# Two interleaved attention layers on one core: a quarter of the numerator tiles multiplied straight out of PSUM

## The chip, the core and the metric

The kernel runs on one core of a Trainium2 chip. Its time is the device time of one execution in microseconds (us); before the change the median of three runs is 454.13 us (452.84 to 454.67). Beside the runs there is one profiled execution, with a record of every instruction. In its views PE is TensorE's matrix product and PEld its load of weights, DVE is VectorE, ACT ScalarE, POOL GpSimd and SP the engine that only issues DMAs. D names the PSUM tiles.

## What is computed

The input x has 2048 tokens of 512 numbers. Two layers, A and B, are applied twice in turn, each to a layer norm of x and with its result added to x:

```python
x = x + _A_ref(_layernorm(x), ...)   # round 0
x = x + _B_ref(_layernorm(x), ...)
x = x + _A_ref(_layernorm(x), ...)   # round 1
x = x + _B_ref(_layernorm(x), ...)
```

Layer A is attention with 32 heads of 16 in four segments of 512 tokens; from the second segment on, each mixes masked softmax attention within the segment with a memory of the segments before. Layer B is linear attention, where the change lies:

```python
phi_q = concatenate([softmax(pq), softmax(-pq)])   # 32 features from 16 per head
phi_k = concatenate([softmax(pk), softmax(-pk)])
kv  = einsum('bhsf,bhsd->bhfd', phi_k, v)          # over all 2048 tokens
z   = einsum('bhsf->bhf', phi_k)
num = einsum('bhqf,bhfd->bhqd', phi_q, kv)
den = einsum('bhqf,bhf->bhq', phi_q, z) + 1e-06
o   = num / den                                    # then o @ wo
```

Because kv is a sum over all tokens, no query of layer B can be finished before the last key of the round is done.

## The kernel before

The 2048 tokens are 16 tiles of 128, four to a chunk. `Kernel.build` (lines 1143 to 1177 hold its loops) writes down, for each round L, the norm and projections of layer A (`a_proj`), its attention (`a_att`), the output projection (`out_proj`), the norm for layer B, and layer B's keys and values (`b_keys`), segment by segment; then `b_query` for each chunk c. At the end of round 0 the queries of layer B run beside the norms and projections of round 1; at the end of round 1 they are the last thing in the kernel.

Each step becomes an operation in a graph: one matrix product of a tile, one activation, one vector instruction or one DMA. Nothing is scheduled while the kernel runs. `Graph.place` (line 157) unpacks `ORDER`, a compressed table that holds three things: the order of all 2904 operations, the engine of each one that could run on more than one (an evacuation of PSUM can go to ScalarE or to VectorE, `evac`, line 358), and the buffer of each of 1479 tiles. `Graph.emit` (line 190) gives each engine its operations in that order, and puts a wait on a semaphore wherever an operation needs another engine's result or a buffer that is still in use. So an engine whose next operation is not ready stands still, whatever lies behind it.

PSUM is cut into four tiles D of 128 x 1024 32-bit numbers (line 447). Every product of every stage goes through one of these four, and one comes free when the last engine that reads it is done.

`b_query` treats one chunk. In short:

- Two projections BQ (TensorE), each followed by two exponentials `qexp`, of q and of -q (ScalarE, 1024 columns each).
- The sums of the softmaxes and the denominators (`Zq` on TensorE); from these the weights of the numerators, by small steps that go to and fro between the engines: `zlA` (two on ScalarE), `zsy` and `zsd` (VectorE, lines 1091 and 1092), `zlB` (two on ScalarE), `zsw` (VectorE, line 1095).
- For each of the four tiles t a numerator N (line 1106): 16 small products into one D tile, 1024 columns, a half for q and one for -q. ScalarE copies it to SBUF in 16 bits (`Nev`, line 1116) and VectorE multiplies the copy by the weights (`nmul`, line 1117).
- The two halves are added (`nadd`, line 1123) and the sum is transposed by a DMA, or TensorE adds and transposes at once (`otp`, line 929) and the result is evacuated (`ote`, line 933). The set `PE_T` says which.
- The output projection and its addition to x (`res`, line 961) for two tiles together, or for one where `SOLO` says so; in round 1 the store follows.

Which way the numerator takes is set by one line: a tile in `COPIED` (line 1200) is copied first; the other branch (line 1120), which no tile uses before the change, multiplies it out of PSUM.

Most activations are recorded under line 351 (`act`), evacuations under line 359 (ScalarE) or 360 (VectorE), products under 326 and 341, transposing DMAs under 364.

Of the kernel before, what the change touches and what calls it, by code (L numbers as in the profile page):

```python
# [1206 lines left out]
c-q~01GFVsvUWsl@4UXZY}>YNSC?&@UAAr8?6Pg!w(WYE=T=W+diBh#f4zULd71ZQ=FYuCUwjcK^W3<=APJ-ZfO=3L2pT{`Xav!rF*Jdu&<vVGa)<%(AU;%sEKnUPKmsTU60$=nr~#!R8?=Cy&<YgP  # L1207
gxpXODnTJA47s2+w1F~E3)(_is0{5OCX|DOPy~uXd*}eQp%@?(hgk3vl!p?~5n@9f=mec15hR8jkQ1svUFZd=AT?O%0(l@Qe1&iD9jd}h2!vPQKnV1P*U$$HyoWR}2-3np0PG6=;V~fggE!C@y1`%=
0?FVBaOe&LAP?rnx9|Zz!Y3FB`S54x0TUoU_JpaJ3x`5(45EzS2ZX=CbX*71Fqj6SfEhRkp29O2gySIyEWLvgm<e*Tx$qobz<MZ&pJ5n`h7Hgc`(X%$(i9j4#jrSzfG@BZ9EuE^U@8p8d61QDgsm_f
hM*s9hEg~Uw!s#NPW^E<tc23&PYjpBcE}2|U?R?d0k{J+tOAZRVG;&nI+zZVF$kAH3>pI`VKr31DJan5L@0*^aTyfFLRbVVVlWoKH82#*V}2-$r=bk4g~GTTD&YzkhI4T^#-z#^3}ay)j)MRgfs<e_  # L1210
j>O4u5ca}8JOmC#q<yd-65%Kepu-S?k!Tkjhgh^5XX8%TgEKKP#-_;RhqG`#?1m&*0QSIm9F3V_3~E%k2$tYtoP!Op2`<8gSPdKE0!$B0F&eDE>Ub9B<3Ti-3Zsz3Q?L?u&;%Td3t=1<WJ_@w9>OZP
lTu?N{0VDdN=SoMu`$NMHCPj)!g<(7YcVRFg9{KBS5kdU&uU?9tcwev9yZ7Q6c01NDoTKXR0mt&8Q6#|u^G0)P1qWb;|W}k8_*w;Vg!tjNAVc8!M1n+{4o@x(Nzee!x(@O@fz%+v$zejv4j{2&*2f=
j9alC?xv%#1!G`ZTum3@612zt7#+hf4y~aG)B$(mDm;U`FeV;>19%!&<1g3|f5ua|9Ft=~$OqY34z>>K(sD|P8Q4k8!#d##3WXh5i1onj*cqc@3aml(=sb48)|8iZ#S7SmT2ePmNl~yBUBt*34I5HT
T1>|vAFD<6sS$O@RMZofP+``9im<qpnv!8J+(Q{zTk4H_=>%kAwJ9F;!ThWp)uC$?pDtl+%*n1(drC-M=rUZ!q!bIUKoaUq8|Vslq7Jl?I?@nIk4>lrHKU<4jBevYyamJQDqf+cbO)PLW4eY{X$0NH
u5=wAVFtX1-Do7;z-*Wa6Vo%yj+yZ$KE{HS1)t+B%z?e=2^M8Ns5=#+-gF<+VNV)Q11TdGrlmBF#?k{^Mx$s9^`X(!kNQ&rT1$Ot06oQ$bRB-7!8C{t(F9sYhbb+UqMvCZt*0Y2i8j+wDoqDy6HTUr
w1qxkPE13IC;~i$H}nWT;#+!wx#<&z!B;H6GPA9ej6UNn%0u5U9TlP5w4Gj2UOGjm=`|gvZFGl@(HFc+muL!=q096dBf=9pN%`q1<zgr30-d3$bdk=|O}IhR=m5J(Z}A{|i65v0J*NBg3bU|x_>rbl
K6*syX)YCG@9_=3pbRvRvf@hunok$lcbY*(sQ`VW2Xv8rqT-a17SJK~kdo73Hk0nrJ3{Kf-qRp<jy_XIHjBRF05+JNCr$%dCVEC$s2Dw`D~w1`3d#$NuCi-P(pS39zR(a>mVgaq`<NnR<!L`F$Ffp6
noSib8xiZuj<L)X2{dJ=Zmc{rbe#2I71&5Ng7swG*>E<R{mh0j#zwIlY$5e#y;w!M$xg6J)R*;VCs}3c!;Y{V)Q??aM_F+;hK*&HSuT>i1pA2;&q?=KNw$aGXL}iEH=qpb#O|<4>=qO3F1yWMG0D!d
Mf94TXLHyic8)z}57=B*mc3wes0#VBhwLS*N&##h3uLEQH40+$nPQqRV1{c}n$=>}X(2O=bIVRM!OyS>><O#QCbFk&3JYeTtPY#XLRdw1A11Ld_5da`hfQOPS!FhxEn#(8XXeLdv8AjFo5^OdMQl1-
&LXg7>?anPtzhF=L}vL)R)s}j<C()(v0bbbYruB1s%$m;z#6iTtR@TK?^q)i$Xl@Y><fFwKCybNC2Pz+v-<2gi@?9KRt$L%_v67lj7Md_-!OmPnyq1PSqwIluVvNPEFP0JV-fju{tF}ioi%4OcqCqq  # L1220
H)SFG8>`OB^CoOE-@+IV<x_ZdzLmvdk@+?jg>Ppycm>{;MddYlMIM{2W9?Wi9*wVOwfP1Xhppvx_(m3&{lYh~GCUsJ!OHSTY%?p)6S3P+pI7Gb*&V3I>+)*63NOK<u>@=<o6Qrm=&S+Xz~}HvyasE?
f8y;~BVLu4;*I%6-iAfzO?XMZiI?Up`DPx2ui^>WRGy4a<1zVMo}AC)N!Uc5f-mArcxt|bPvYBnN<N=&=V|x?o`5grU3o0NoOk0p`7*wcC*;XlBEFQb<|}wpo|2_t&G;IglqKd@cq(?4uj8rNdft-9
=B;=#)|qeNTX_=Rg~#E|`7WM@#pNydZhnZTW%2l7o|ebwy?JY%j<w?*cpKiGC*?hPTmCaY#`p2#yd%%VqriUNgZJWhcqe|B_vP(*AAW=P<C*zQ-k+c11NaGknrG!%_&|P=AK}?}Dt?ro;ko!Deit6|
?ED@K;<@=Ao`dJ%2l!yVmmlQ!_z-@U-{+V3d48E+<k$FUUXWksWB5@1l#k`N_ys<WKjF7|AwG<c=Q;Uso{pd6BY0u{fKT8Lc^)y6=jG3MKAxUG=cD)*@q*_S1^7$8Rpb+|cz*tx=NB3H7oL&7;oF21
Z~0fgUA*H;eB<wVi1^Mwa4kM^5JnW?C`dRWRD9xof{CKsiqD*j9YTmO;V%-1ouU{I5D7(~NF{<rA`w9Zi6kPmNGu|XG$NKrDk6zpGMR`XB8%8!mxwBIh-e~?h#_{%=wi2sDN=~IBDvTjQ;K*Zt;i|j
i@h?P$RTry^dhUsCUVN$BBRJIGK);2fXE_p$wDH7C@cz!{bG+OBKC>ga<3>Yii!%Nj3_3Gi|V3;$RiJklH#B!B`S(TqO7<g^2!>bk~l2NiL0Wf*e1)1Bcig%Cu@nH#CCa9)E4<=9dS$)lm%p6aZTJ5
g=ArQUEC5?L_Kjs6p^<@eNj~ul?_BOc}MJ!$3->KP}~(KL~C(I?39f}6LD4?lx;*)v0pY8%|vP0T$GX3Wm|DTwh-+^Cs9MT6#L{o(OI+?hh!JgL$nedL|1WN6qko(Pti?u6ura|*<F;7y+s9iRQ@dH
iaw&EJSX~!d7_^<FHVYMvZU-UE{Nl@l$<Y4i8}Iu7$EA()8d}2DF=$BVu7e6@5^hlmK-fUi|ewotS!&UF=CK7F9(Z@qOAN$juk`25K&Jq6y@Y%@kP89U&S|3UY?Z8#3^}6EEnn3WszNFP~$`n^-e4i
UDbDyTD=#~MK?8Gd=MZXikvEqsv_&l7viH>A#$ll;)G1A7Ky5If_N;_sVCx-7@}T^VPckeDyE1Aa;T~%Uy06Yw&<dsiPs{V%Bym#Iii5dr}C&lDvNp}@~gorv&yOpswT3K%A|UzjB1p6AbYBYvalMh
PRn7ckz6T?sNrh0I3vfY$zqLYuf{8X*;F=`t3(HNR`yZ>a-!(1F39d`sz5nST$IDb&#I#$`A}YxBSa@PRZUcr#6T4&AIUz7$pLDNnxgutv1)|sCP#_BYNV>9jJzyw$jWNEn6LV)4zj3PpysM8QptHr  # L1230
${C`nx+*8ANvfJErY5W6>L=Ao#*))i6*XNwmRgolT+S3vWOpfK2~}FfmQQ6#HBz*eR@PQCRT))Q%~BOq9N9)zR5esvSzRquj;yI_sXFRsxk!~)&15-MUDs8ivWBjw{N!TQQMQveWo^Agg~?~KzN(`)
hzN46*eK%4Uqk}ANko<FL<!wqK9>pQ8~H+Zk|lLC8K7UvTe5*lBm;GG>8GR1AnmW0s>HIPiYSA13mHScm8JAMxlA=uDdc-uTE~=~<!qHw_K=O$9JN_2S4~t;nM$ryujE>lOtw@_)f#nMHdDW-<Py{-
wMr$CcVuL_StXUha<wA8Lfw_UB-86ubCpG|SL+4WU1V07TDDTzWNRgK1{p~P$&50J1l>kulI?X@`AMRVq(gN?ZFD@@LC2RHR7<IKn3mdVM@P^~Z&V?Ai;AqH=&fppYOA&>R6EsYnO*Ku?NnX;MQ&Gv
^jEoC4c4TXdM%6Ty{ewxulA`us<%9#ifgXY$q+e0_mLy@LDf(Xmwja;onEGqiFE~?R`!!g^awdn&QKNgXEjpR)L+zcc}UgLA7nW_Kz>tSRefDve^)DH3)Mi+mn-EU*;xOio9QMxs&1-B%QCv7E~^*F
Xu6YbrJL)8^04|SN68|3usos`$)b9Q6sn~jrjM!?dbqBvE9s>An2N2F=}YRkI-^dgI6AsMsjBHJ`mBnfzsZ>TvO1+=>2vD5I<2benew`7tuLr6s*O&rZ>U-Fq8cNws?<8APN7rj*|NJ%sK3j2`e&U+
r`2)wD4js}mx=Uf9bc!@h4eC+Uf)w0^c>kk7uG{`Pkmnv)fshH{ZKtnnRGWD&pc9@WqdPNE|zWeIDJh`)Q{D8y-MCxPt+3mOtsVV<XAaD_tRtaSUpZo)z8&<*;y}@lXVvz$4t^w^aPn%$2F7WMA=LC
(L?1e)mvvUS@ctt(Ol4dbyj^*574*tK;2*8)_3$|c~Ac$r|G*|s_A;Iysz`<OM11eZ!YV{I-6Fifyt|9=yN)s*6OCduJh~j`l+6&Z|Gd+p?;#T=|?)Zd7xjYY$k`fqO+T;+Fw1>Yh+GyM`ba?<Z~UM
vYOW_nF&;}OmZ_z$2KSRZI#4WHCvz3NzEIT&rFeXbUO1^r8n7iLGw~2Fgf%)byuC%3C$~&$fPy-O=4qICX>d@)j4$mliFl9smyy-+te|2O&${mrpgbho|z`ed{pyv0nJPaGha`apHxZnM(5Ib%>unx
pV4o1N|Rfk)hWz39i*bFLgu?(sKG>2FLYsprl5YOm+0tfom{Hl>sNZ2UN2|J*SeJ1AY+*2y0j7IqmHShS*c^16*`9cpc@)x9Q8$i)s0MJ<EK{XMY@UEBtL0wKI>mJH=AXsTCKOpbvl+Zrlwh=tqD`L
jAJU92&$N=Y+9IBrnqTpf>jOE+!QetOf%EcY?Nh;pDAjpn~G+;j;tc7vSzI=XLjiF=B19P+L(`KkFI8-sMh9_scJT8e^bSTsGm%1wNtk>dv!Y#Xm{y2YO4&g?af;gS7oprOk$PMemCz-5*1H@U1^f4  # L1240
1!jv`XjYl!W}i-ESD0j~quFZK>#t^!S!xp7P9}lctrMzmW{ZxmI-6xCk#g)-okIE9jrzTLZMNwE^TvEIpG|TVXnLAd>Wf)yQmP=c%d9qQ%r9o0S!*_!-DabSWHy=2CbG$7dzmGsw^?ttnLZ}7-D!51
P#eW;H^Ii(Fw1RUBdxVjO&1fv3fs>x+tqB+5v{+CW&&)8*<+&FU>j<p+vsMm2{Tb_h()_uA2MVkm@M|7?q(v{!=}55Y9pEhW}i_utBq{;>oZ2%{pO&FVGrw=_N+OikC<%sh(2l#=<N1_IjYZ@^X9ZU
W-gh_=D3MvFPb>^XLHhAF*$5p8{76bIqg+*&BU`k%n5VKTsQG;E_=faFgHzZo50>O$8<uQ%-%M~b#gn}oX|r|0h`YbHF<0rJIv&@1??C!&<rw#>>V@K3^pn3U6ax#vG+`2o79doY3+TJ-i|j9%v1Bw
q_&UDWRu@MHWN%bo60^j&&@>h#C)<ZOc6WW6tz>#ep}4GG{x;_JIR!=uS_NT#ZEOPZDl*ce6^+QPxgQ<ZKs*qwu(JytJ>zajICx5+3L2etz*mC@^-qJWh&SPwuY^1N0}D3qOE6Vn3{IB8EI<ShPJ*v
Z0DF(wvlaVkJy=}wQX#h*q*kHZEEM5cD9#oX6Ko<wzr*V``SMCsGV;H+ex;)J!ZSuPPT&`Vkg_qwx8{4r`nFTn;mF}+Wxk?9bl)}X?BnuW`DNR?K|7U&alJndpp98vJ>n$`@xQ}W9=L}-p;bK?Pz<_
ezeE!NITP_1I}E#&Cavm?J2w6ezWuK0=v;Jv@0z+C+s52oW*vN<<1Tp$ysHSIKtU!H(Ti}v8U}Wo77otm2<{McDC5F?$=;|v(#?237ja-8XM?Dcb3_N&RQG8IcK9f#tCw)v)e{<Vmjxo<1Dv{oIQ4h
P3FXMezAT|VrQ?7?X0sGY;xzK^>?n@U?-)M%2{u3*woG?8{(vJF58<nj&sYVah}>MHm;M_d1i0hbk0?q*(v3ucd|I~oE*+Io56WtpWBR1sFTyl<m|IA>_Z#oWOZKJTux~xn{&rLve}*7&SQJmMsV^t
Pi#RauT#b;<lM7moqSF?C!$l>iSOihUfKJ$h_k`Iwnd!+PI>2zE#_2kiaQmZx3+{+$tmd|N6tBO_kZ4)yAgRG@?E(bAcb$tyY-I+?h(;9`TLV^bI<Vi8+xk|eyDbj5Pkp%H}&iJ4>LXoU6~)}-&T=t
3MhR4{k6|i{?ErBlITf7xP`yE^Q)ylSagHKe+2luYgh8`rvB*6k6HW+3H)oN|JKq!83FVG9gZmeaY*oY@Zj&j!2b{)gulV)??C$J0O;Qj{yzcgUm!*Q2~xi<@<D>XAN&cQ|7Ki%P~eY4^zQsOMD@E2
{(A9SHT)wMq~BEv{dxTB=81)W!V4q3`N59^{5HVfO#S8QPc`<Z0{gAa{juHswRsPXa6JDo`1i{DUv<C#6$kzw+V8*Rz;EY&vvTS0D)+y$;r~S&`#;c}@&8y<zxAL0%GQeiUs|hAJO4wS^MBO{{x_C;  # L1250
v4_XZe{J~uA9uW+dC#lJ5SZ^N7npEom_qH|bQp!}^d6uMLk8|MI73n>wea&t3RXygEQ|sG{DcHfexAMX=j!mMF!C7<3HId^Tovx_bxi~b7C0JDz%v~{LEuXU^ZY^d7p^CgN%kW<0HLUuLq6@qQG+Dm
# [45 lines left out]
```

## Time and profile before

| | before |
|---|---|
| median of three runs | 454.13 us |
| the runs | 452.84 to 454.67 us |
| the profiled execution | 452.45 us |
| its span, first to last instruction | 450.7 us |
| TensorE busy, weight loads apart | 426.8 us |
| weight loads busy | 283.0 us |
| ScalarE busy | 421.6 us |
| VectorE busy | 399.4 us |
| GpSimd busy | 58.5 us |
| granted TensorE clock | 1.00 |

A busy time is the union of an engine's instructions. Products are pipelined and their ends are modelled, so TensorE's figure is not a measure of how near it is to its peak. The chain, a view of its own, is followed back from the last instruction: at each step to whatever released it, or else to the instruction before it on its engine. A group is all instructions of one line, engine, operation and shape, with their number, their total and the mean of one in ns. In a row of the timeline, several alike in succession are drawn together (x3), with the time from the first's start to the last's end. The 32 numerator copies run at 204 to 231 us (round 0) and at 419 to 443 us (round 1), and the multiplies at 206 to 251 and 421 to 444 us.

### The profile page before, as it was taken

How to read it: one execution, taken by the hardware profiler on the slowest of the kernel's cores; microseconds unless marked ns; L12 is line 12 of the kernel's file. 1: busy time of each engine (PE TensorE's matmuls, PEld its weight loads, DVE VectorE, ACT ScalarE, POOL GpSimd, SP SyncE). 2: the span in 40 equal slices, each digit the busy share in tenths (PEclk: the TensorE clock that was granted, in tenths of full speed). 3: DMA queues.
4: the chain of work that ended last, by engine and by line, in shares of the span. 5: the costliest groups of instructions: out<-in, count | busy, mean ns of one | idle time of the engine just before them, and what ended most of it. 6: DMA issues, size and time to landing. Idle time of an engine off the chain costs nothing.

```text
span 450.7 us, 26149 instructions
## 1 busy us (share of the span) xinstructions
PE 426.8 (95%) x12085; PEld 283.0 (63%) x12085; DVE 399.4 (89%) x764; ACT 421.6 (94%) x586; POOL 58.5 (13%) x146
## 2 busy tenths in 40 slices
...
GB/s 252 214 168 54 129 122 98 96 109 76 61 71 97 37 46 33 31 1 16 26 109 114 85 97 110 78 98 83 60 34 56 102 50 63 28 25 4 38 97 188
DMA packets 105167, 36.71 MB, mean 81 GB/s; under 512 B 91730, under 2 KB 105058, under 8 KB 105058
## 3 DMA queue, kind: packets, MB, share of 16 engines
...
q0 software_dynamic: 32, 0.02, 0.0%
...
## 4 chain that ended last, share of the span: by engine, by line
PE 53%; ACT 29%; DVE 11%; DMA 3%; issue 2%; POOL 0%; SPq 0%; DVEq 0%; POOLq 0%
PE D L341 35%; PE D L326 18%; ACT p L351 16%; ACT pP L351 11%; DMA p<-p 2%; DVE stats L599 2%; DMA X<-in_A_x_dram 1%; ACT pS L351 1%; DVE pQ L686 1%; DVE X L961 1%; DVE p L1117 1%; DVE pK L360 1%; DVE p L620 1%; DVE p L360 1%; DVE p L675 1%
## 5 line engine op out<-in xcount | busy, mean ns | idle before, releaser
L351 ACT ACTIVATE p<-D 128x1024 bf16<-128x1024 f32 (+1 forms) x256 | 226.2, 939 | 8.5 <-PE D L341 5.0
L351 ACT ACTIVATE pP<-D 128x768 bf16<-128x768 f32 (+2 forms) x192 | 150.4, 831 | 6.2 <-PE D L326 4.9
L326 PE MATMUL D<-pK,pQ 64*128 64x256 bf16 (+6 forms) x1792 | 110.8, 227 | 5.5 <-ACT pP L351 1.6
L326 PEld LDWEIGHTS D<-pK,pQ 64*128 64x128 bf16 x1792 | 64.1, 94 | 39.9 <-ACT pP L351 8.9
L326 PE MATMUL D<-pW,pP 64*128 64x50 bf16 (+1 forms) x3072 | 84.9, 181 | 1.3 <-ACT pP L351 0.5
L326 PEld LDWEIGHTS D<-pW,pP 64*128 64x128 bf16 x3072 | 68.5, 93 | 9.4 <-ACT pP L351 1.4
L607 POOL TENSOR_SCALAR rstd<-mv 128x1 f32<-128x1 f32 x60 | 16.7, 282 | 337.2 <-DVE mv L600 337.2
L326 PE MATMUL D<-pW,p 64*128 64x50 bf16 (+1 forms) x2048 | 49.2, 181 | 0.1
L326 PEld LDWEIGHTS D<-pW,p 64*128 64x128 bf16 x2048 | 43.4, 93 | 3.9 <-ACT p L351 0.5
L599 DVE BATCH_NORM_STATS2 stats<-X 128x6 f32<-128x512 bf16 x63 | 42.3, 681 | 1.9 <-DMA X<-in_A_x_dram 1.4
L961 DVE TENSOR_TENSOR X<-X,D 128x1024 bf16<-128x1024 bf16 (+1 forms) x36 | 39.4, 1098 | 3.0 <-PE D L341 2.7
L326 PE MATMUL D<-tri,rep 64*128 64x64 bf16 (+1 forms) x384 | 39.2, 197 | 0.0
L341 PE MATMUL D<-pX,WA_q 64*128 64x512 bf16 (+1 forms) x288 | 37.5, 353 | 0.2
L341 PE MATMUL D<-pX,WA_k 64*128 64x512 bf16 (+1 forms) x288 | 37.1, 353 | 0.5
L609 POOL TENSOR_TENSOR rstd<-rstd,mhalf 128x1 f32<-128x1 f32 x60 | 36.3, 608 | 4.0
L1015 DVE TENSOR_REDUCE pS<-p 128x64 f32<-128x1024 bf16 x28 | 33.4, 1210 | 1.6 <-ACT p L351 1.6
L341 PE MATMUL D<-WA_o,p 64*128 64x512 bf16 (+1 forms) x288 | 32.9, 353 | 1.8 <-ACT pP L351 1.0
L341 PE MATMUL D<-WB_k,pX 64*128 64x512 bf16 (+1 forms) x288 | 33.5, 353 | 1.0 <-ACT pP L351 1.0
L341 PE MATMUL D<-WB_o,p 64*128 64x512 bf16 (+1 forms) x288 | 32.9, 353 | 1.3 <-DMA p<-p 0.5
L341 PE MATMUL D<-WB_v,pX 64*128 64x512 bf16 (+1 forms) x288 | 33.2, 353 | 0.2 <-ACT p L351 0.2
L341 PE MATMUL D<-WA_v,pX 64*128 64x512 bf16 x256 | 32.9, 377 | 0.1
L341 PE MATMUL D<-pX,WB_q 64*128 64x512 bf16 x256 | 32.2, 377 | 0.1
...
## 6 DMA issues: line engine op xcount, KB each, us to landing
...
p<-p SPq DMA_TRANSPOSE x73, 3.2
pX<-p SPq DMA_TRANSPOSE x54, 3.7
...
```

What stands on the lines that cost most here:

```text
L326: ins = e.matmul(out_ap, lhsT, rhs, start=st, stop=sp, tile_position=(basep(lhsT), basep(out_ap)))
L341: ins = e.matmul(out_ap, lhsT[64 * hf:64 * hf + 64], rhs[64 * hf:64 * hf + 64], start=k == 0 and i == 0, stop=k == 1 and i == len(lists[hf ...
L351: return self.g.op({"act": (dur, lambda e: e.activation(out_ap(), in_ap(), func, scale=scale))}, reads, writes, opens, label=label)
L360: "dve": ((340 if fast else n / 0.96 + 65), lambda e: e.tensor_copy(out_ap(), in_ap()))}
L599: v(lambda e: e.bn_stats(self.stats[:, t, :], self.X[:, t, :]), 602, [R("X", t)], [R("st", t)], label="bn")
L607: v(lambda e: e.tensor_scalar(rs, self.mv[:, t, 1:2], LN_EPS, None, op0=ALU.add), 170, [R("mv", t)], [R("rstd", t)], eng="pool", label="rstd")
L609: v(lambda e: e.tensor_tensor(rs, rs, self.mhalf[:], ALU.pow), 540, [R("rstd", t), R("mhalf")], [R("rstd", t)], eng="pool", label="rstd")
L620: v(lambda e: e.tensor_scalar(xn.t[:], self.X[:, t, :], self.mv[:, t, 0:1], self.rstd[:, t:t + 1], op0=ALU.subtract, op1=ALU.mult), 300, [ ...
L675: v(lambda e: e.tensor_tensor(cut(dst), cut(dst), cut(e_), ALU.min), 68 + n / 1.92, D + E, D, label="phadd", port=True)
L686: ch = {"dve": (129 + n / 3.84, lambda e, sl=sl, out=out: e.tensor_scalar(out(), src(), self.m4[:, sl:sl + 1], None, op0=ALU.mult))}
L961: self.v(lambda e: e.tensor_tensor(X(), X(), src(), ALU.add), 65 + 512 * n / 0.96, pr + xr, xr, label="res")
L1015: v(lambda e, E=E, k=k, Z=Z: e.tensor_reduce(Z.t[:, 64 * k:64 * k + 64], E.t[:].rearrange("p (a f h) -> p a h f", a=16, h=4), AX.X, ALU.ad ...
```

## The change

Of each four numerator tiles the last is taken out of `COPIED`. The eight tiles 3, 7, 11 and 15 of both rounds now take the branch at line 1120: no `Nev` and no copy in SBUF, and `nmul` reads D.

```diff
-COPIED = {(L, t) for L in range(2) for t in range(16)}
+COPIED = {(L, t) for L in range(2) for t in range(16) if t % 4 < 3}
```

The two ways, as they stood and stand:

```python
if (L, t) in COPIED:
    Ns = self.T(self.p2, "T")
    self.act(lambda Ns=Ns: Ns.t[:], lambda N=N: N.t[:], ACT.Copy, 1024, [N], [Ns], label="Nev")
    v(... e.tensor_tensor(shape(Tm.t[:]), shape(Ns.t[:]), w(), ALU.mult) ..., label="nmul", port=True)
else:
    v(... e.tensor_tensor(shape(Tm.t[:]), shape(N.t[:]), w(), ALU.mult) ..., label="nmul")
```

The rest of the diff replaces `ORDER`, 52 lines of text, with a table for the 2896 operations and 1471 tiles that are left. Unpacked and set beside the old one, with the eight copies left out, it has the same operations in a slightly different order: 401 of TensorE's 1165 stand at the same place in its queue, 302 of ScalarE's 569 that both tables give it, 101 of VectorE's 755. The mean shift is 2.3 places on TensorE, 0.9 on ScalarE, 4.9 on VectorE and 2.9 on SP; 1039 of the 1471 tiles get another buffer of their pool. Seventeen operations change their engine (times are those of the profiled execution before):

```
to ScalarE:  ote of tiles 1, 2 (round 0) and 0, 14 (round 1); K of round 1, segment 0 (235.6 us);
             Q of round 1, segment 1 (248.7 us); one accumulation of the memory (263.6 us)
to VectorE:  K of round 0, segment 2 (67.4 us); K and V of round 1, segment 1 (248.8, 270.5 us);
             layer B's V in round 1, three times (362.6, 387.1, 403.3 us);
             one evacuation of a transpose (394.4 us); one mask of K (12.9 us)
to GpSimd:   two memsets of the setup (1.9, 39.2 us)
```

In the last stretch of the kernel the order of the numerators' steps on VectorE becomes, from the first weights on: tiles 3, 1, 2, 10, 8, 11, 0, 9, 5, 7, 4, 12, 6, 13, 14, 15 (before: 3, 2, 1, 10, 0, 9, 11, 8, 5, 4, 7, 12, 13, 6, 15, 14).

More of the change, by code (lines that the diff above doesn't have):

```diff
@@ L1206 @@
 ORDER = """
[L1207 to L1250, printed above, removed]
@@ L1255 @@
-?k9-(nCGGHl9@utbvD!`pmDf6$6Phipuct#=2FAur=RyO3f85G8&RMSBws!-{FT$yBP{-)qA#<;4bNCt7r9jg-n%BFU<$(!aPS8e!AN()-^JI529j~@IvC(_&!ZM-5#ac0ED*v8qCEW`OT9mjgu%Y0
-KEk<o1R1Wvn09Fq#=@1jQW_i<>;>$}xCP*HIMij0^l9*fT@o8N!0=Ewx|t92no6MbaY!(K@PX~C2hUXz;wkdIL;Ezk*F1oQdhV0IuOi*lg}H?SDADJz%fBEuJhw#rJSKT7LOpi4*n1`H`5{Fp_jnQH
-2w&#W@u~K>;R{-@A2jzAcwoA1%lJVsy5;Oc&({e8K)EdEgg<@=Fu^X*1H5GTq`}{<+YmRYzAq8-x}U30yP0F;6}hX__bY>c2m}PX^S~igyU>9v;b;m~#%mc67>2&E$+bin>b5rHqD=lmY7Ag*jBYq?
-xue?vf|S3+0C(Va70|{_1q*gd&8-D4{K%0Qgob;~(5*SwnsCkk4-Bs7x&
+c-rlEWwhkVt*%Nc_U65ZnVFfHnVFfHXU;G)Gcz+YGcz+Y^USk*&q>Zn@^X{4@_yv5=We@PE=eVQ`lNQpfD{0b9P&d-s1F1ZvI0T_P|y%8B!Whe3m7zpoZvtchzW6_Da3=^&<sjK2qb~%&>Rv&AQXgB
@@ new lines @@
+&;qhU1*i@NvOr771EoPgD<}jtpf!|%n$QL~<b$@54GKe9Xa}(%8We%{5FctmMTiYWApj~tIp_ezpf*&7j!+(wK_{pK#i0sxh7!;PK0;mS3iY5W^oH+H4Sv9DNCn;CC!~fx04xo>fdr5i-hzg~z*t|%
+1fL)wAR7P!p*!@0A<!QNK~ne(PvIT(fFKwOdDtlU0{NI9{04bhPk09Jp%+YJ7N0|YmW#cB_3#05Q*M?6GQ&%l!KSkf5QMMbE6ikr*hrWQ8(}aj!RA49EXg*(aOlS-!Z(--6CfCuKz}wLim_=B8AiZp
+m;^&uaW)Jx!gkmUb6_Z&4yD)*I1Q!QGML0>z*g7^#AZPZ%t~8e09yrlXdBE1&hpYgwi<RpOmuK21Tuf{!!b|*mckmC!X`6+6f78mSS*~%LU1oEhqX|E6=j9kSSZ3OuzgUFS+)+!u)?e&E60M_9w^U-
+v9fG8tbpOH5}U_X!hBYljbP(oBpVNtVLyumQ{XThV3LhuXJJ1C;1M_g>0mS~NQu}52w_Jd8|`HWVHVRYG26$|!yI-7X0x&EJQO0s#;~Q#VRKnSmV_-}OIRQ_Volj1wwNu3W~@3>Y$b~dHCRME%oehf
@@ new lines @@
+u!^N(u`wx&ghyB?+l5tF1{lZu*aSA7?Z!ngkyT}paT!a^0$3DW&Z@D()R+~aG^{3T!s4)eREve;3bvLVz;$dPT!gr60bGJ}a1d8vJXVj@Va-_s)`qRdR;(^-%{H@^EGpJ#wOI=mhFjQ17RI9CCU%mw
+Wk*>%c8VQm`6&X6&l0fq>^NM9V=N*&1UKLW+sY!b9V{i=#`fR^mYkhqd+``thCM6}uEEG`JB!X@unz1BM8LHeh3#esSw|L=9b)NeHA}(HvQF$gTf@?_(`-Epg)?je%RmX)3XIL_VP}?+R$_Lli8<&u
+wv+8*^|1@<$=YC7c9HdB-B>M5#xAi|*cMY_Z*~e=<7L(e`>-V#mDR=u*chX+RM?j-#Z1%?<6>$&0sF8Hc4zys9oEHo*n_pl8yFw2u$$=5I$&4qf=MtTUWKdd8pL9o@EU819dR=b#ZK56o8vHSiNmo8
+W@OjdV>SZQvm5L#yM{Me2G#<b;Vm{2uVXiS!tTI5)*bJ&QTTvmW0}|s_K;;~nb}j8gB8Rq>?M1|GE;AS#&S|mEQGgNA54VlSX%6b<1qq^!@{@>$KV|{2$$mo9Eg2!G>*jq*aQ3HI_!rDup~Zbzu|fu
@@ new lines @@
+f`jo0Zor9n6iZ<doP=3uBPPXTxD_YkaXf^HaSI;CWH<%4;U`ua)8IS&%-&-<ybX_GJAP+RAUA$tuUHEF!R}xl{L1cP0eXXZaR=_iGx!!y;ypZzCGZ61WcTq3eq&Ry7+%HV_zZK=X#{+Zr|=S<!)bUK
+&*Lr3$_~+OoR05VQB019=^_4PPw*3dVEHgVrpKc68DF!HtQh^o0{99u;9K?@FW@DL2tP0*KElgX2A|>=JVLkND;}jc>;pc)ckD5K#Ex_kXW(G!L<1=+4k3<+gNX12zC?!CNZ?G&j@M}x-XMwJ@FoqV
+@0bOL(E(BjR2~l!qjFRhD<D!f>_+qO1eHULMBS-889Yhzu_rCS3N)HV(Lx+Uy=Wx$pb^xEexu=Zi!xzFtVFk|63)g`R2lox06I;*DF+^-E7X^cQ-8{g#c3?%#H%!pBridWQ1LK$KqV;`?xTmapE#AJ
+#n_qdQC_%1rAg3znuB+#480*q=jkm)fk!l#=Hf*<NApP0E2@eY=rO&f`SgUU;Tc*$)o~&Dlje)4HfahVLxx-8{3)HKKoZ=ci4;W7s17}+Ni>y$DU_yBT?(O!^bjUf7(Ie1bQ3DmQtCp>C^Ai_uC#<^
```

43 lines of the change are left out of this document (39 added, 4 removed).

## The prediction

> **What bounds the kernel now.** I read the page's busy times and its chain first, then a table of windows, the chain in order of time, the groups of instructions, and single stretches of the timeline.
>
> ```profile
> PE 426.8 (95%) x12085; PEld 283.0 (63%) x12085; DVE 399.4 (89%) x764; ACT 421.6 (94%) x586; POOL 58.5 (13%) x146
> ...
> PE 53%; ACT 29%; DVE 11%; DMA 3%; issue 2%; POOL 0%; SPq 0%; DVEq 0%; POOLq 0%
> ```
>
> Three engines are nearly full, and no one of them sets the end alone: the chain runs 53% over TensorE, 29% over ScalarE, 11% over VectorE. What ScalarE loses is worth time only where the chain lies on ScalarE, and what VectorE gains costs time only where VectorE has no slack. So the next view is the table of windows, cut where the change acts (columns: window and length, then busy us of PE, PEld, DVE, ACT, POOL).
>
> ```profile
> 60.00:80.00 20.00, 18.93 (x544) 13.86 (x538) 17.98 (x38) 19.56 (x28) 6.93 (x14) 1.00 0.78 111
> 200.00:214.00 14.00, 12.09 (x412) 7.57 (x408) 11.15 (x27) 13.89 (x23) 0.00 (x0) 1.00 0.06 12
> 214.00:228.00 14.00, 13.30 (x326) 7.46 (x324) 13.76 (x31) 14.00 (x23) 3.31 (x8) 1.00 0.29 43
> 252.00:300.00 48.00, 46.82 (x1387) 32.00 (x1380) 41.74 (x84) 47.08 (x60) 9.64 (x24) 1.00 0.58 93
> 380.00:410.00 30.00, 30.00 (x710) 18.71 (x708) 23.89 (x39) 26.16 (x42) 3.13 (x8) 1.00 0.18 30
> 421.10:448.20 27.10, 24.25 (x528) 13.31 (x528) 26.61 (x47) 21.40 (x32) 0.00 (x0) 1.00 0.58 120
> ```
>
> The two query stretches of layer B, where all copies of the change lie, are about 200 to 252 and 415 to 448 us. At 200 to 214 ScalarE is full (13.89 of 14.00) and VectorE is not (11.15). At 214 to 228 both are full. In the last 27.1 us VectorE is the fullest of all: 26.61, or 98%. At 380 to 410 it is TensorE (30.00 of 30.00).
>
> **What each piece costs.** From the groups by line:
>
> ```profile
> L1117 DVE TENSOR_TENSOR p<-p,pS 128x1024 bf16<-128x1024 bf16 x32 | 21.4, 686 | 0.4
> L835 DVE TENSOR_TENSOR p<-D,pS 128x1024 bf16<-128x1024 f32 x12 | 14.6, 1217 | 0.9 <-PE D L326 0.4 <-ACT pS L351 0.2
> L360 DVE CAST p<-D 128x1024 bf16<-128x1024 f32 x10 | 12.2, 1221 | 1.1 <-PE D L341 0.9
> L360 DVE CAST p<-D 128x512 bf16<-128x512 f32 x7 | 4.7, 679 | 0.1
> L359 ACT ACTIVATE p<-D 128x512 bf16<-128x512 f32 x6 | 3.6, 596 | 0.6 <-PE D L341 0.4
> L359 ACT ACTIVATE pT<-D 128x1024 bf16<-128x1024 f32 x7 | 7.1, 1037 | 0.0
> L688 ACT ACTIVATE pQ<-p,m 128x512 bf16<-128x512 bf16 x2 | 1.3, 723 | 0.0
> L553 DVE MEMSET pW<- 128x1088 f32 x1 | 1.0, 965 | 0.2 <-issue 0.2
> ```
>
> And from the timeline of ScalarE, three numerator copies in a row, and the first of the last query stretch among its neighbours:
>
> ```profile
> 206.02 2.84 ACT L351 ACTIVATE p<-D 128x1024 bf16<-128x1024 f32 x3
> ```
>
> ```profile
> 417.87 0.38 ACT L351 ACTIVATE pS<-D 128x256 f32<-128x256 f32 x1
> 418.29 0.42 ACT L351 ACTIVATE pS<-pS 128x256 f32<-128x256 f32 x1
> 418.76 1.02 ACT L351 ACTIVATE p<-D 128x1024 bf16<-128x1024 f32 x1
> 419.68 0.30 ACT L351 ACTIVATE pS<-pS 128x128 f32<-128x128 f32 x1
> 419.88 0.38 ACT L351 ACTIVATE pS<-D 128x256 f32<-128x256 f32 x1
> 420.14 0.61 ACT L351 ACTIVATE pS<-pS 128x128 f32<-128x128 f32 x2
> ```
>
> One copy lasts 1.02, but the next begins before it ends: (2.84 - 1.02) / 2 = 0.91 us is what ScalarE gets back for each. VectorE's multiply took 686 ns from SBUF. Before shows none with a numerator in PSUM; the nearest row is L835, the same operation and size with its large operand in PSUM: 1217. I take 1217, so + 0.53 us for each.
>
> **Part 1: eight copies gone.** ScalarE 8 x 0.91 = - 7.3 us; VectorE 8 x 0.53 = + 4.2 us; the wait of a multiply for its copy goes, and a wait for the product itself takes its place. Queued behind that wait on VectorE are, in the table of after, the next tiles' multiplies and half-sums, and behind the last one four residual adds; for these wait the transposes of SP and TensorE, the output projections and the stores.
>
> **Part 2: engines that the new table moves.** Unpacked, the two tables differ in 17 engines. From VectorE to ScalarE go four evacuations of 512 columns (tiles 1 and 2 of layer 0, 0 and 14 of layer 1) and two of 1024 (K at 236, Q at 249 us); from ScalarE to VectorE six of 1024 (K at 67 and 249; V at 270; layer B's V at 363, 387 and 403). One costs ScalarE about 0.5 or 0.9 us, VectorE 0.6 or 1.13 (the rows less an overlap of 0.1). ScalarE: 2 x 0.9 + 4 x 0.5 - 6 x 0.9 = - 1.6. VectorE: 6 x 1.13 - 2 x 1.13 - 4 x 0.6 = + 2.1. Small pieces (a mask, L688, and a 512-column evacuation go to VectorE, an accumulation to ScalarE, a memset, L553, to GpSimd, which is 13% busy) take about 0.7 more off each. Whole kernel: ScalarE - 10, VectorE + 6, TensorE 0.
>
> **Part 3: order and buffers.** TensorE keeps 401 of 1165 steps in their place and the others move by 2 or 3 on the mean (22 at most); ScalarE's by 10 at most. SP's transposes and loads move by 3 places on the mean (some weight loads of the first 60 us by more), GpSimd's setup memsets change places among themselves ahead of its first normalisation step; in the last query stretch two stores go ahead of transposes on SP, which costs nothing, as VectorE's queue has their residual adds ahead of the half-sums that those transposes wait for. I cost the reshuffle at nothing, because the same steps stand in the same stretches; its bounds are in the range. It is the least known term.
>
> **Where it lies on the path.** The chain in order of time, at the places concerned:
>
> ```profile
> 65.88 1.02 ACT p L351
> ...
> 68.01 1.04 PE D L341 x8
> ...
> 210.16 2.74 ACT p L351 x3
> ...
> 214.42 1.17 DVE X L961
> ...
> 362.87 0.96 PE D L341 x8
> ...
> 418.76 1.02 ACT p L351
> ...
> 426.13 1.99 ACT p L351 x2
> ...
> 434.72 1.87 ACT p L351 x2
> ```
>
> - *K at 67 us.* The chain leaves ScalarE for TensorE at 68.01, ScalarE is the fuller (19.56 against 18.93 of 20): between 0 and 0.9; I take half, - 0.45. V at 363 likewise, on the border from TensorE (362.87): - 0.45.
> - *V at 387 and 403, the evacuations at 236 to 270.* Hidden behind TensorE (30.00 of 30.00; 46.82 of 48.00). Nothing, so long as VectorE's slack there (6.1 and 6.3 us) takes them; if it did not, 1.13 us each.
> - *First query stretch.* The chain holds two removed copies (210.16, x3): - 1.8; two 512-column evacuations come to ScalarE ahead of the same point: + 1.0. From 214.42 the chain is VectorE's, which has + 2 x 0.53 and - 2 x 0.6 by then. ScalarE's bound is - 0.8, VectorE's - 0.1; I take - 0.5.
> - *Last query stretch.* ScalarE's bound: three copies on the chain (418.76, 426.13, 434.72), 3 x 0.91 = 2.7, less 0.5 for the evacuation that comes over: - 2.2. VectorE's bound: 4 x 0.53 - 2 x 0.6 = + 0.9 on an engine at 98%. But VectorE also begins earlier:
>
> ```profile
> 420.48 0.43 DVE L1095 TENSOR_TENSOR pS<-pS 128x256 bf16<-128x256 f32 x1 [0.99 <-ACT pS L351]
> ...
> 421.15 0.69 DVE L1117 TENSOR_TENSOR p<-p,pS 128x1024 bf16<-128x1024 bf16 x1
> ```
>
> It stood idle 0.99 us for weights whose last step on ScalarE was queued behind the copy at 418.76. Without the copy that step comes some 0.4 earlier (a second chunk's two steps, 0.2 to 0.6, now go ahead of it), and more of VectorE's small work is done in the gap: 0.7 to 1.0 us. So + 0.9 - 0.9 = 0 for this stretch; the later of the two bounds, VectorE's, decides.
>
> Sum: - 0.45 - 0.45 - 0.5 + 0 = - 1.4 us. The profiled execution took 452.45 us (span 450.7, 1.75 around it), 1.7 below the median shown, 454.13; the same step from the median gives 452.7. What a measurement of this kernel can tell from no change is about 0.5%, 2.3 us, so the forecast is a small gain inside it.
>
> [...]
>
> **Rivals.**
>
> A. *ScalarE's relief pays wherever the chain is on it.* The full terms: - 0.9, - 0.9, - 0.8 and - 2.2 make - 4.8 us: 449.3. At its far end all of ScalarE's 10 us come off: 444. For it: TensorE's waits below, 7.2 us in these three rows alone, end on ScalarE. Against: VectorE's 98% at the end.
>
> ```profile
> PE D L326 <- ACT p L351: 3.1, 9, 0.5
> PE D L326 <- ACT pP L351: 2.1, 9, 0.4
> ...
> PE D L341 <- ACT pP L351: 2.0, 3, 1.0
> ```
>
> B. *VectorE becomes the bound in the query stretches (slower).* A numerator now holds one of four PSUM tiles until VectorE's queue reaches it. The multiply is longer and stands behind residual adds (L961, 1.17 us in the chain above), and TensorE's next product waits for the tile. Price: the + 4.2 of the eight multiplies, with the 4 x 0.6 of evacuations as a credit or, if TensorE then waits for ScalarE's, without it: + 1.8 to + 4.2, up to 458; at the middle, + 3: 457. It decides once VectorE has no gap left to absorb 2 us in the last 27 (it has 0.5 now). Against it: the table puts VectorE's multiplies close behind their products.
>
> C. *The copies are not on the path and nothing moves*: 454, as TensorE's 426.8 us are untouched.
>
> **Chances.** My case with C, -3.4 to + 1 us around - 1.4: 0.46, of which 0.12 lies beyond 0.5% faster. A: 0.32. B: 0.20, of which 0.02 is under 0.5%. What is left, that the change doesn't do what it says, 0.02, counts as the same. Faster by over 0.5%: 0.44; within: 0.38; slower: 0.18. The likeliest case's own range is 450.7 to 455.1. The range for 8 in 10 reaches into A to 447.5, past its 449.3 by the 2 us that the order may give, and into B to its middle, 457.0.
>
> **What would show it.** ScalarE's busy time near 411, VectorE's near 405, TensorE's at 427. L1117 as two forms: 24 of about 686 ns, 8 of about 1217 reading 32-bit D. In the last 27 us VectorE at 98% or more, and the chain there passing from ScalarE to VectorE: right. A chain still on ScalarE there and a span down by over 4: A. TensorE's waits on L1117 or L961 over 3 us in the query stretches: B. A multiply from PSUM far from 1.2 us, or a difference that sits outside the query stretches, makes my working wrong whatever the time.

## The result, and the profile after

After takes 450.06 us (median; 448.93 to 456.62, but for one execution of 687.42 us at a granted clock of 0.56), before 454.32 us (450.17 to 456.8) beside it. The ratio is 0.992 [0.989, 0.994]: faster by 0.8%, 3.8 us, and the interval leaves out no change. The profiled execution took 449.23 us against 452.45, with a span of 447.5 us against 450.7.

The page's busy times and chain:

```profile
PE 426.6 (95%) x12085; PEld 284.3 (64%) x12085; DVE 404.1 (90%) x763; ACT 413.1 (92%) x577; POOL 57.5 (13%) x148
...
PE 63%; ACT 20%; DVE 13%; issue 2%; DMA 1%; DVEq 0%
```

ScalarE lost 8.5 us and VectorE gained 4.7. The chain's share on ScalarE fell from 29 to 20% and went to TensorE. The groups of copies and multiplies:

```profile
L351 ACT ACTIVATE p<-D 128x1024 bf16<-128x1024 f32 x184 | 183.7, 1041 | 7.7 <-PE D L341 4.0 <-PE D L326 3.1
L1117 DVE TENSOR_TENSOR p<-p,pS 128x1024 bf16<-128x1024 bf16 x24 | 15.9, 684 | 0.0
L1120 DVE TENSOR_TENSOR p<-D,pS 128x1024 bf16<-128x1024 f32 x8 | 9.8, 1220 | 0.0
```

The eight multiplies out of PSUM took 1220 ns each (1217 was the estimate). The same windows as before the change, the last one again the 27.1 us up to the last addition to x:

```profile
60.00:80.00 20.00, 19.85 (x538) 14.02 (x539) 19.02 (x35) 19.06 (x28) 3.56 (x7) 1.00 0.77 110
200.00:214.00 14.00, 13.15 (x428) 8.29 (x430) 11.60 (x22) 13.97 (x24) 0.85 (x3) 1.00 0.13 22
214.00:228.00 14.00, 13.62 (x282) 7.39 (x278) 13.79 (x30) 13.93 (x22) 2.38 (x6) 1.00 0.36 81
252.00:300.00 48.00, 46.76 (x1380) 32.29 (x1372) 42.92 (x87) 46.61 (x61) 10.24 (x24) 1.00 0.55 96
380.00:410.00 30.00, 29.77 (x686) 18.95 (x680) 27.27 (x47) 23.42 (x37) 3.15 (x8) 1.00 0.15 25
418.20:445.30 27.10, 23.78 (x512) 12.78 (x512) 25.78 (x42) 18.58 (x30) 0.00 (x0) 1.00 0.58 118
```

TensorE is fuller at 60 to 80 us (19.85 against 18.93) and at 200 to 214 (13.15 against 12.09). In the last stretch VectorE is not fuller but emptier, 25.78 against 26.61. The chain there, in order of time:

```profile
416.89 1.24 DVE p L1120
418.57 1.20 DVE p L1117 x2
421.06 1.01 ACT p L351
422.27 1.83 ACT p L351 x2
...
431.03 1.83 ACT p L351 x2
433.85 1.05 PE D L341 x8
...
440.62 2.19 PE D L341 x24
442.83 1.82 DVE X L961 x2
```

It begins with a multiply out of PSUM on VectorE, goes to ScalarE and from 433.85 us to TensorE's output projections.

Where the time came from is read by laying the two traces over each other: for each operation of ScalarE and VectorE, its end after less its end before, and of these the median in each 20 us. The lead of after is 0.2 us at 20 to 40 us, 1.1 at 40, 1.9 at 60, 2.9 at 180, 3.1 at 200, 3.9 at 240, 3.6 at 300 and 3.3 at the end. So in this pair most of it stood before the first numerator. The experiments were built on that; how far a single pair can be trusted is seen at their end.

### The profile page after: what moved, and what is told of

Read it like the earlier page. It is cut to its first block, busy times and chain, and to the rows that moved or that the text cites. A ratio compares the mean times of both kernels' runs of the same rounds, so it can differ in the third digit from the quotient of the medians.

```text
span 447.5 us, 26142 instructions
## 1 busy us (share of the span) xinstructions
PE 426.6 (95%) x12085; PEld 284.3 (64%) x12085; DVE 404.1 (90%) x763; ACT 413.1 (92%) x577; POOL 57.5 (13%) x148
## 3 DMA queue, kind: packets, MB, share of 16 engines
q8 instruction: 95, 1.56, 1.4%
## 4 chain that ended last, share of the span: by engine, by line
PE 63%; ACT 20%; DVE 13%; issue 2%; DMA 1%; DVEq 0%
PE D L341 39%; PE D L326 21%; ACT p L351 13%; ACT pP L351 6%; PE D L701 2%; DVE X L961 1%; DVE pQ L686 1%; DVE p L360 1%; DVE stats L599 1%; ACT pS L351 1%; DVE pS L1015 1%; DVE p L675 1%; DMA pX<-p 1%; DVE p L620 1%; DVE p L1117 1%
## 5 line engine op out<-in xcount | busy, mean ns | idle before, releaser
L351 ACT ACTIVATE p<-D 128x1024 bf16<-128x1024 f32 (+1 forms) x248 | 217.1, 931 | 11.2 <-PE D L341 7.2
L326 PEld LDWEIGHTS D<-pK,pQ 64*128 64x128 bf16 x1792 | 65.6, 93 | 40.5 <-ACT pP L351 8.1
L326 PE MATMUL D<-pW,pP 64*128 64x50 bf16 (+1 forms) x3072 | 83.6, 181 | 1.2 <-issue 0.7
L326 PEld LDWEIGHTS D<-pW,pP 64*128 64x128 bf16 x3072 | 67.5, 93 | 6.4 <-issue 1.1
L607 POOL TENSOR_SCALAR rstd<-mv 128x1 f32<-128x1 f32 x60 | 15.8, 272 | 338.4 <-DVE mv L600 338.2
L961 DVE TENSOR_TENSOR X<-X,D 128x1024 bf16<-128x1024 bf16 (+1 forms) x36 | 39.0, 1094 | 4.0 <-PE D L341 3.4
L609 POOL TENSOR_TENSOR rstd<-rstd,mhalf 128x1 f32<-128x1 f32 x60 | 35.2, 596 | 2.7
```

The source lines that it names most:

```text
L326: ins = e.matmul(out_ap, lhsT, rhs, start=st, stop=sp, tile_position=(basep(lhsT), basep(out_ap)))
L351: return self.g.op({"act": (dur, lambda e: e.activation(out_ap(), in_ap(), func, scale=scale))}, reads, writes, opens, label=label)
L607: v(lambda e: e.tensor_scalar(rs, self.mv[:, t, 1:2], LN_EPS, None, op0=ALU.add), 170, [R("mv", t)], [R("rstd", t)], eng="pool", label="rstd")
L609: v(lambda e: e.tensor_tensor(rs, rs, self.mhalf[:], ALU.pow), 540, [R("rstd", t), R("mhalf")], [R("rstd", t)], eng="pool", label="rstd")
L961: self.v(lambda e: e.tensor_tensor(X(), X(), src(), ALU.add), 65 + 512 * n / 0.96, pr + xr, xr, label="res")
```

## The experiments

A kernel was put together from the two tables, by order, engines, copies and buffers. Each comparison is with before on the same chip in the same session (453.0 to 455.7 us), so ratios are compared. The theories were: T1, the new order and engines ahead of the query stretches make the gain and the edit nothing; T2, ScalarE's eight copies make it; T3, the edit costs time on VectorE and the order overpays that.

**1. The edit alone, in the old order.**

```diff
 order and engines of before; 48 tiles in other buffers; 6 steps put off for want of a buffer
-32 copies
+24 copies
+the product N of these eight tiles 2 to 7 places before its multiply, where it stood 9 to 111 before it
```

> The edit alone: the eight tiles are multiplied out of PSUM, but order and engines are those of the old table. (The product of a tile that stood more than eight places ahead of its multiply is moved to six places ahead of it, 6 steps are put off by a place or more until a PSUM tile is free, 48 tiles get another buffer.) Theory 1, the gain of 3.8 us is the new order and its engines in the first 197 us, ahead of the first numerator, and the edit is worth about nothing: 453 to 456 us, the last 27 us on VectorE unchanged or up to 1 us longer. Theory 2, the gain is ScalarE's 7.3 us of copies: 449.5 to 451.5. Theory 3, the edit by itself costs time on VectorE and the order overpays it: 456 to 458.

463.85 us, 1.021 [1.016, 1.026]. Slower by 2%, more than any of the three theories expected; T3 is the nearest, as TensorE now waits for the new multiply:

```profile
PE D L341 <- DVE p L1120: 2.9, 3, 1.2
```

**2. The new order and engines, with all copies.**

```diff
 order and engines of after; 50 tiles in other buffers, 8 more for the copies
-24 copies
+32 copies, the eight 2 to 4 places behind their products
```

> The edit undone: order and engines of the new table, but all 32 tiles are copied by ScalarE again; each of the eight copies is put four places behind its product in the order. Theory 1 (the order ahead of the first numerator): 449.5 to 451.5 us, no slower than the changed kernel by over 1.5. Theory 2 (the copies): 453 to 455. Theory 3 (the edit costs): 447 to 449.5, faster than the changed kernel.

457.54 us, 1.007 [1.003, 1.011]: slower than before, and 1.6% above after. This speaks against T1: with all copies put back like this the new order is no gain.

**3. The new table up to the first query step, the old one from there, all copies.**

```diff
-order and engines of before for the first 1360 operations; buffers
+those of after; 53 tiles in other buffers
```

> The first part of the new table alone: its first 1360 operations, up to the first denominator product of layer B in round 0 (about 197 us; the old table has the same operations there but one), then the old order and engines, with all 32 copies. Theory 1: most of the gain, 451 to 452 us, and the span up to the first numerator shorter by 2.5 to 3. Theory 2 and theory 3: 453.5 to 455, and the lead of the first part lost again behind ScalarE in the query stretch.

457.27 us, 1.004 [1.000, 1.008].

**4. The old table up to there, the new one and the edit from there.**

```diff
-order and engines of after for the first 1360 operations; buffers
+those of before; 64 tiles in other buffers
```

> The second part of the new table alone: the old order and engines for the first 1360 operations (about 200 us), then the new order with the eight tiles out of PSUM. Theory 1: 453 to 454.5 us, a gain of 0 to 1. Theory 2: 450 to 451.5. Theory 3: 455 to 457.

454.34 us, 0.998 [0.995, 1.002].

So each mixture lost the gain, and none of the three theories says that. The profiles of runs 2 and 3 have something that they do not mention. Both execute the first 1360 operations in after's order on after's engines, and yet TensorE stood still in the middle of a product, waiting for nothing that the profile shows. First the timeline of run 2, then its windows (busy us by engine as above, then the granted clock, the share of the DMA engines and GB/s):

```profile
60.75 1.02 PE L341 MATMUL D<-pX,WA_q 64*128 64x512 bf16 x7
65.19 0.39 PE L341 MATMUL D<-pX,WA_q 64*128 64x512 bf16 x1 [3.42 <-issue]
```

```profile
60.00:62.00 2.00, 1.40 (x20) 0.59 (x15) 1.97 (x5) 2.00 (x4) 1.97 (x4) 1.00 1.58 251
62.00:64.00 2.00, 0.00 (x0) 0.00 (x0) 0.67 (x2) 0.38 (x2) 0.00 (x0) 1.00 1.74 114
64.00:66.00 2.00, 0.81 (x27) 0.77 (x29) 0.00 (x0) 0.10 (x1) 0.00 (x0) 0.90 0.34 69
66.00:68.00 2.00, 2.00 (x25) 1.54 (x21) 1.60 (x2) 1.41 (x2) 0.00 (x0) 0.50 0.04 8
```

After the gap of 3.42 us the clock stood at 0.50. In run 3 the gap was 3.46 us, up to 66.84, and the clock stood at 0.50 from 66 to 70 us. By the tables run 3 has after's buffers too in these 1360 operations, so the same stretch of program ran with the gap in the one profiled execution and without it in the other. In after the eight matmuls run through:

```profile
60.28 1.54 PE L341 MATMUL D<-pX,WA_q 64*128 64x512 bf16 x8
```

The queue of instruction transfers, q8 in the DMA view, shows the other half. In before, after and runs 2 and 12 it counts 95 packets and 1.56 MB, 16 KB each; TensorE's 24,170 instructions (12,085 products and as many weight loads) make 254 for each, so I take q8 to be TensorE's refill. That is my estimate from these counts: no view names the engine. In after one falls in the window from 55.7 to 60 us, starting at 59.01. In run 2 none falls in 56.7 to 61.8. The queues' rows of these two windows (packets, MB, share of 16 engines), after first:

```profile
q1 hardware_dynamic: 896, 0.59, 57.4%
q8 instruction: 1, 0.02, 1.4%
```

```profile
q1 hardware_dynamic: 1560, 0.97, 100.5%
```

There the data queue had the engines at 100.5%, with a 512 KB load of layer B's weights among it (it stands in after's window too, issued at 57.22 us), and the refill started at 61.88, while the eighth matmul began only at 65.19. In each of the five such gaps of runs 2, 3 and 8 to 10 TensorE went on 1.3 to 1.4 us after the end of the late refill's packet, which bears this reading. T5: it is this collision that made the mixtures slow, not what they were made of. It does not account for run 4, whose profile has no stand of this kind over 0.9 us.

**5 and 6. Engines without order, order without engines.** The other two came out of the same question: which part of the new table is it?

```diff
 run 5: order, buffers and 32 copies of before
-17 operations on their engines of before
+17 operations on their engines of after
```

> The order, the buffers and all 32 copies are those of before; only the 17 operations that the change puts on another engine are on it. If the engines are what was gained ahead of the query stretches (K at 67 us and another early product off ScalarE): 451 to 452.5, with the lead of 1 to 3 us there by 200 us. If they pay only with the order that was made for them: 454 to 457, since nothing stands where the new engine is free. My guess is the second, 455.

457.63 us, 1.009 [1.006, 1.012].

```diff
 run 6: order, buffers and 24 copies of after
-17 operations on their engines of after
+17 operations on their engines of before
```

> The order, the buffers and the edit are those of after; the 17 operations are on their engines of before. If the new order alone carries the gain ahead of the query stretches: 450 to 452, the lead of 3 us still there at 200 us. If the engine changes carry it: 453 to 456, with the lead gone from 67 us on. By theory T2 (ScalarE's relief) it is slower, since the moves of the query stretches put work on ScalarE that the edit has freed: VectorE then keeps the two output transposes and three scalings, +1.8 us on VectorE in the first query stretch.

456.35 us, 1.003 [1.000, 1.006]. Neither half pays by itself. The first query stretch, 196 to 252 us, suggests why, though a fixed window holds slightly different work in each kernel; before, then run 5, then run 6, then after (PE, PEld, DVE, ACT, POOL):

```profile
196.00:252.00 56.00, 52.74 (x1362) 31.59 (x1360) 51.25 (x112) 55.36 (x78) 6.59 (x16) 1.00 0.37 61
```

```profile
196.00:252.00 56.00, 51.94 (x1338) 30.78 (x1340) 47.56 (x102) 55.80 (x79) 6.59 (x16) 1.00 0.41 61
```

```profile
196.00:252.00 56.00, 51.79 (x1348) 30.69 (x1344) 51.60 (x106) 51.36 (x71) 6.19 (x16) 1.00 0.38 60
```

```profile
196.00:252.00 56.00, 53.56 (x1428) 32.53 (x1424) 51.65 (x104) 55.14 (x78) 6.13 (x16) 1.00 0.38 65
```

With the engines moved and the copies kept, ScalarE is full (55.80 of 56) while VectorE has 8.4 us free. With the edit and the old engines ScalarE has 4.6 us free and TensorE does less work. With both, the work that went to ScalarE fills what the copies left, and TensorE does 1.6 to 1.8 us more in the same window, 0.8 us more than before.

**7. The control for run 1.**

```diff
 order, engines and buffers of run 1
-24 copies
+32 copies, each 1 to 3 places behind its product
 one multiply changes places with its neighbour
```

> The control for the edit alone in the old order (463.85): that kernel's order, with the numerator's product moved late, its put-off steps and exactly its buffers, but with all 32 copies, each some three places behind its product. It differs from the edit alone in the eight copies and nothing else. If the multiplication out of PSUM is what cost the edit alone its 10 us: 453 to 456 here. If the late products and the other buffers cost it: 460 to 465.

463.28 us, 1.019 [1.014, 1.024]. Run 1 by run 7: 1.002 [0.995, 1.009]. In this order, the old one with the products moved late, the edit shows no gain and no cost, to within 0.5 and 0.9%; what cost run 1 its 10 us is what I had built around it. T3 has lost its evidence. The edit in before's order as it stood was not run.

**8. The control for run 2.**

```diff
 order, engines and 24 copies of after
-buffers of after
+buffers of run 2 (50 tiles)
```

> The control for the new order with its copies put back (457.54): the kernel after, with exactly that kernel's buffers (50 tiles in other buffers than after). It differs from it in the eight copies and nothing else. If the copies cost it its 7 us against after (theory T2 within the new order): 450 to 451.5 here, as after. If the buffers cost it: 455 to 458, and the mixtures so far say little about copies or order.

453.96 us, 1.000 [0.997, 1.003]. Other buffers alone take after's gain away. Its timeline has the gap at the same matmul, and the refill started at 61.96 us:

```profile
64.45 0.39 PE L341 MATMUL D<-pX,WA_q 64*128 64x512 bf16 x1 [2.05 <-issue]
```

**9 and 10. The load moved away.** Run 9 is run 8, run 10 is after, with one DMA at another place:

```diff
 SP's queue
-load (wqkv, 512 KB)
 PhKtr L0 s1 gp1; vsw L0 s1 gp1; otr L0 s0 i02 gg1; xnT t1; xnT t0
+load (wqkv, 512 KB)
```

> The kernel after with the other buffers (453.96; the profiled run 451.40) with one DMA moved: the 512 KB load of layer B's weights that went out at 57.55 us stands five places later in SP's queue, behind the transpose of 64.5 us. New theory T5: that load kept back the 16 KB refill of TensorE's instructions that is due at about 59 us (it started at 61.96, and TensorE stood 2.05 us with nothing to wait for, 3.4 us in two other runs), and the buffers as such cost nothing. T5 expects 450 to 451.5, no gap of TensorE over 1 us at 62 us, and the refill at 59 to 60 us. If the buffers cost their 4 us through waits of the engines: 453 to 455 as without the move.

> The kernel after, with its own buffers, and the same load five places later. By T5 the profiled run of after was on the good side of that collision (load out at 57.22 us, refill at 59.01 us, no gap), and most of its runs too: 449 to 451, as after (450.06) or a little under it where some of its runs were caught. If the load's late landing (about 70 us, its transposes are issued at 70.65 us) holds something back: 451 to 453.

Run 9: 450.75 us, 0.994 [0.991, 0.997]; run 10: 450.81 us, 0.995 [0.991, 0.998]. With the load moved, the other buffers cost nothing that shows: run 9 by run 10 is 0.999 [0.995, 1.004]. The move itself made the kernel of run 8 faster: run 9 by run 8 is 0.994 [0.990, 0.999]. The refill of run 9 started at 58.04 us, but the gap did not go, it moved with the load; this is the timeline of run 9, and run 10 has the same 1.42 us at 72.30:

```profile
72.10 0.31 PE L326 MATMUL D<-pK,pQ 64*128 64x128 bf16 x6 [1.42 <-issue]
```

**11. Before with other buffers.**

```diff
 order, engines and 32 copies of before
-buffers of before
+54 tiles in other buffers, 27 of them in those of run 7
```

> The kernel before with 54 tiles in other buffers, order, engines and copies untouched: about as many as the edit alone in the old order had (48 to 49). If the buffers cost the edit alone and its control (463.85 and 463.28) their 10 us: 460 or more here. If it is the late products that cost it: 454 to 456, and what is above 454 is the price of buffers not chosen for the order.

455.79 us, 1.006 [1.003, 1.009]. Of run 7's 1.9%, 0.6 may be the buffers, though only 27 of its 49 moved tiles stand here as there; the rest, 1.3% [0.7, 1.9], is then the late products and the steps put off.

**12. The copies back in the new order, without the gap at 62 us.**

```diff
 order (with the load later), engines and buffers of run 9
-24 copies
+32 copies
```

> The new order and engines with all 32 copies (457.54, where TensorE stood 3.42 us at 62 us and its clock fell to half for 3.4 us behind that), with the same 512 KB load five places later. It differs from the run with other buffers and the load later (450.75) in the eight copies and nothing else, and neither has the gap at 62 us. So it prices the edit within the new order, free of that collision. Theory T2 (the copies' time on ScalarE, 8 x 0.91 us, is on the path): 453.5 to 455.5, the loss lying at 200 to 240 us and behind 410 us. If the edit as such is worth nothing (T1): 450 to 451.5, and the whole 7 us by which the copies lost before were the gap and the clock.

458.34 us, 1.006 [1.004, 1.009]. Run 12 by run 9: 1.0125 [1.008, 1.017], so the eight copies cost 5.6 us [3.8, 7.5] in the new order; runs 2 and 8 differ by the same edit and gave 0.7% [0.3, 1.2], 3.3 us. T2 expected such a price, within the new order. The first query stretch and the end of run 12 against run 9, run 12 first:

```profile
196.00:252.00 56.00, 51.33 (x1341) 30.45 (x1335) 46.55 (x99) 55.64 (x79) 6.13 (x16) 1.00 0.37 60
410.00:460.00 50.00, 37.80 (x912) 21.38 (x908) 36.89 (x72) 35.30 (x54) 0.00 (x0) 0.94 0.36 74
```

```profile
196.00:252.00 56.00, 52.21 (x1338) 30.99 (x1331) 50.08 (x102) 53.73 (x76) 6.13 (x16) 1.00 0.34 63
410.00:460.00 50.00, 32.56 (x858) 18.97 (x852) 34.05 (x62) 27.96 (x43) 0.00 (x0) 0.95 0.35 73
```

ScalarE is full again (55.64) with VectorE 9.4 us free, and behind 410 us ScalarE has 35.30 us left to do instead of 27.96. It is here that run 12 falls back: laid over before, run 12 is 2.2 us slower from 200 to 240 and 3.5 from 400 to 440, run 9 0.5 and 1.3. So the expectation placed the loss rightly, and its size a little low.

But T2's mechanism, ScalarE's time, is not all that the copies bring here. VectorE's multiplies in run 12:

```profile
L1117 DVE TENSOR_TENSOR p<-p,pS 128x1024 bf16<-128x1024 bf16 x32 | 21.4, 685 | 9.4 <-ACT p L351 9.3
```

VectorE stood 9.3 us waiting for copies, 5.0 of them in the first query stretch; in before the same row has 0.4 us, and in run 9 L1117 has none and L1120 1.0. The new order puts these eight products only 2 to 11 places ahead of their multiplies (before: 9 to 111), so a copy put back between the two has no time to run ahead. In run 7 the wait is 5.5 us, and there the edit gains nothing, so it need not cost its length. How much of the 5.6 us is ScalarE's time and how much this wait, no run separates. The granted clock is not the cause: run 12's four executions at 1.00 took 456.2 to 461.1 us, run 9's seven at 0.999 or 1.00 448.8 to 451.3.

It also takes something away from T5. Run 12 differs from run 2 by the moved load alone, and the ratio is 0.999 [0.995, 1.004]. The gap is real in the profiles and follows the load, but what it is worth over many executions lies between nothing (runs 2 and 12) and 0.6% (runs 8 and 9). The single executions of run 8 lean to the second: three at a granted clock of 0.999 or 1.00 took 451.4 to 452.4 us, the other nine, at 0.995 or 0.996, 452.9 to 456.6 and once 459.1, while run 9's five at 0.995 or 0.996 took 449.1 to 452.1. That is not settled.

How far a single pair of profiles can be trusted, promised above: runs 1, 4, 7 and 11 have before's order and engines up to 190 us, and laid over before, runs 1 and 4 are 1.9 and 1.2 us behind it at 200 us, runs 7 and 11 1.8 and 1.6 ahead. After's lead of 3.1 there (run 10: 2.5, run 9: 2.5, run 12: 1.5) is at the edge of that. That the early part gains is likely, not shown.

## Why the prediction was right or wrong

The time, 450.06 us, lies in the range (447.5 to 457.0) but not in the likeliest case's own (450.7 to 455.1), and faster by over 0.5% had 0.44. It stands nearer to rival A's 449.3 than to the 452.7 forecast: that the range holds it is owed to rival A's part of the range, not to the working.

- *Busy times.* Forecast ScalarE near 411, VectorE near 405, TensorE at 427; measured 413.1, 404.1, 426.6. Right but for ScalarE's 2 us.
- *The price of a multiply out of PSUM.* Taken as 1217 from the nearest row, measured 1220 over eight. The prediction looked for it as a second form under L1117; it stands under L1120.
- *"I cost the reshuffle at nothing, because the same steps stand in the same stretches."* This step failed. Order and engines with the eight copies put back cost 0.7% against before (runs 2 and 12), engines alone 0.9%, other buffers 0.6% in the old order (run 11) and 0.8% in the new (run 8 by after). These, 3 to 4 us each, are larger than every term that I summed. What the reshuffle is worth together with the edit, which is what the kernel runs, no run separates.
- *First query stretch, - 0.5.* The pair of traces gives - 0.8 from 200 to 240 us. But the working was for copies gone at the old order's pace. In the runs the copies cost nothing that shows in the old order with late products (runs 1 and 7) and 3 to 6 us in the new one (runs 8 and 2, 9 and 12). In run 12 ScalarE is full there and VectorE is not, but part of VectorE's free time is its wait for the copies. Part 1 names that wait and gives it no price: it is 0.4 us in before, but 9.3 with the copies put back into the new order (run 12). The terms of parts 1 to 3 were added as if each had its own price; the runs show prices that depend on the rest of the table.
- *Last query stretch, 0, VectorE at 98% or more and the chain passing from ScalarE to VectorE.* The time fits (+ 0.3 from 400 us to the end in the pair), the reason does not: VectorE's busy time there fell to 25.78 of 27.10, 95%, and the chain passes from ScalarE to TensorE at 433.85.
- *A difference outside the query stretches makes the working wrong.* Most of the lead of this pair, 2.9 of 3.3 us, stands before 200 us. By the prediction's own test the working was wrong, as far as one pair of profiles can say (its noise at 200 us is some 2 us). The test did not fit the sum: 0.9 of the 1.4 us forecast, K at 67 and V at 363 us, lie outside the query stretches too.
- *Rival A.* Its sum, - 4.8, is near the - 3.8, and the copies' 3.3 to 5.6 us in the new order are of its size, though VectorE's wait for them is in that price. Its test, a chain on ScalarE at the end and a span down by over 4, was not met (3.2). The runs agree with the rival in the new order (0.7 and 1.25% for eight copies) and not in run 7's (nothing that shows).
- *Rival B* did not happen: in the two query stretches TensorE waits 0.2 us for L1117 in all, 0.2 us for L1120 and for L961 not at all, and run 1 by run 7 shows no cost of the held PSUM tile beyond 0.9%. The first reading of run 1, that the edit costs 10 us, was this rival, and only the control told it apart.
